# Decode attention on one core: pairwise additions on VectorE in place of half the score reductions on TensorE, with the statistics of an item moved behind the next item's first multiply

## The chip, the cores and the metric

One core of a Trainium2 chip. The metric is device time in microseconds (us) of one execution. The kernel before took 1992.97 us (median of 3 runs, 1991.46 to 1994.55).

## The reference

Two attention blocks, A and B, of the same shapes, one query token each; the results are put side by side.

```python
B, Sq, D = 2, 1, 640
H, Sk, Dh = 32, 8192, 192
q = (x @ wq)                       # per block; reshaped to (B, H, 1, Dh)
scores = einsum("bhqd,bhkd->bhqk", q, k_cache) * Dh ** -0.5
p = softmax(scores, axis=-1)
o = einsum("bhqk,bhkd->bhqd", p, v_cache)
out = o.reshape(B, Sq, H * Dh) @ wo          # concatenated over the two blocks
```

Everything is bf16. There are 2 x 2 x 32 = 128 pairs of a batch entry and a head. The kernel calls each pair an *item*. An item reads 8192 x 192 keys and as many values, 3 MB each, and uses every number once. 837 MB are loaded in all.

## The kernel before

Items are numbered 0 to 127 and fall into 8 groups of 16. Each K and V tile is 128 partitions x (64 x 192). K has 2 slots, V has 3. One queue (SyncE) issues all loads in order; a slot is loaded again when its former item has been used:

```python
for i in range(NH):                                   # SyncE
    # ... loads of wq and wo for a coming group at fixed items
    if i >= NK: sp.wait_ge(s_mul, NCH * (i - NK + 1)) # all 4 multiplies of item i-2
    sp.dma_start(kslot(i % NK), ...)
    if i >= NV: sp.wait_ge(s_pv, i - NV + 1)          # all value matmuls of item i-3
    sp.dma_start(vslot(i % NV), ...)
```

The scores of an item are formed by VectorE and TensorE together. VectorE multiplies K by the query, in four chunks of 48 of the 192 dimensions. TensorE sums the products by matmuls with an identity matrix that accumulate in PSUM, six per chunk, 24 per item, each folding the sum into 8 partial sums per key. VectorE adds the 8 (`sred_nrs`), takes the minimum of the negated scores per partition, TensorE transposes it (`maxt`), VectorE reduces it to the bias (`bias_op`), ScalarE takes the exponential, and TensorE multiplies by V in 32 matmuls (`pv_range`).

```python
def mul_chunk(i, c):                                  # VectorE, K x q for 48 dimensions
    # ... c == 0: wait for the K load
    if ci >= NP: dve.wait_ge(s_red, ci - NP + 1)
    dve.tensor_tensor(out=pslot(ci % NP)..., in0=kv[:, :, c*DCH:(c+1)*DCH],
                      in1=qv[...].broadcast_to([P, T, DCH]), op=ALU.mult).then_inc(s_mul, 1)

def red_chunk(p, c):                                  # TensorE: 6 matmuls of 128x512
    pe.wait_ge(s_mul, ci + 1)
    for j in range(MPC):
        mm = pe.matmul(S_ps[p % 2][:, 0:SN], lhsT=ident_b, rhs=pv_[:, :, j*D2:(j+1)*D2], ...)
    mm.then_inc(s_red, 1)

for i in range(NH):                                   # VectorE
    mul_chunk(i, 0); mul_chunk(i, 1)
    if gd is not None: group_end(gd)                  # normalise a finished group
    mul_chunk(i, 2); mul_chunk(i, 3)
    sred_nrs(i)
    bias_op(i)
    if gd is not None: mask_copy(gd)

for p in range(NH + 1):                               # TensorE, cut
    pv_range(p - 1, 0, 16)                            # value matmuls of the item before
    for c in range(NCH):
        red_chunk(p, c); pv_range(p - 1, u, u + 2); u += 2
    pv_range(p - 1, u, u + 4); u += 4
    maxt(p)
    pv_range(p - 1, u, TU)                            # the last 4
    # ... group-end transposes, query matmuls, projection
    # after the last item: pv_range(127, 0, 32), 14 matmuls to keep the clock up, transposes, projection
```

At the end of a group VectorE normalises the outputs, replicates them eight times under a mask (`o_rep`, 32 x 1536 fp32), and TensorE brings them into the layout of the projection by 12 fp32 matmuls against a 0/1 matrix. The profile counts 24 instructions for these.

## Time and profile before

| | before |
|---|---|
| time | 1992.97 us |
| DMA, share of its 16 engines' time | 98% |
| TensorE (PE) busy | 85% |
| VectorE (DVE) busy | 53% |
| loads, steady rate | about 429 GB/s |

Lines of the page of the kernel before: busy time and its share of the span by engine, three strips of 40 equal slices (granted TensorE clock in tenths, DMA share in tenths, GB/s), and the bytes read.

```profile
PE 1701.0 (85%) x8536; PEld 722.9 (36%) x8536; DVE 1058.0 (53%) x1084; ACT 91.0 (5%) x326; POOL 5.4 (0%) x17
...
PEclk9989999999899998999999999899999989999998
DMA  9999999999999999999999999999999999999993
GB/s 402 424 433 427 433 425 431 428 432 429 427 428 431 429 429 428 429 429 430 429 427 429 431 428 431 427 430 429 430 429 428 430 430 430 427 409 429 431 429 139
...
HBM read 836.77 MB, written 0.01 MB: 420 GB/s over the span
```

The DMA strip is at 9 (90% or more) in 39 of 40 slices. GB/s is flat near 430 apart from the first and the last slice and one at 409, which holds the end of the last group but one; we come back to it. These are groups of instructions of the same kernel: line, engine, operation, output and inputs with shapes, count, then busy us and mean ns of one, then the idle time of that engine just before them and what ended it.

```profile
L339 DVE TENSOR_TENSOR pbuf<-kbuf,qbc 128x3072 bf16<-128x3072 bf16 x512 | 866.2, 1753 | 488.1 <-DMA kbuf<-in_A_k_cache_dram 256.7
L514 PE MATMUL bank<-pbuf,ident_b 128*128 128x512 bf16 x3072 | 796.6, 398 | 272.0 <-DVE pbuf L339 272.0
...
L348 DVE TENSOR_REDUCE sc_sb<-bank 128x64 f32<-128x512 f32 x128 | 88.6, 692 | 338.0 <-PE bank L514 338.0
```

VectorE stood idle 488 us until a K tile landed, and 338 us until TensorE had finished a reduction. The loads do not wait for long. The list of load issues (count, size, median us from issue to landing) shows them queued well ahead:

```profile
kbuf<-in_A_k_cache_dram SPq DMA_DIRECT2D x64, 3072.0 KB, 22.5
vbuf<-in_A_v_cache_dram SPq DMA_DIRECT2D x64, 3072.0 KB, 25.4
```

A tile of 3 MB takes 7.3 us by itself at 429 GB/s. It lands 22.5 or 25.4 us after its issue, so 15 to 18 us of other loads stand ahead of it. Now the ending, from the timeline (start us, duration us, engine, line, operation, count, and in brackets the idle time before it and what ended it):

```profile
1941.46 6.76 DVE L339 TENSOR_TENSOR pbuf<-kbuf,qbc 128x3072 bf16<-128x3072 bf16 x4 [4.06 <-DMA kbuf<-in_B_k_cache_dram]
...
1956.07 6.76 DVE L339 TENSOR_TENSOR pbuf<-kbuf,qbc 128x3072 bf16<-128x3072 bf16 x4 [4.06 <-DMA kbuf<-in_B_k_cache_dram]
...
1968.79 5.37 PE L532 MATMUL bank<-vbuf,zwin 128*32 128x384 bf16 x32
...
1975.56 2.83 DVE L392 TENSOR_TENSOR o_rep<-tmpB,mask 32x1536 f32<-32x1536 f32 x1
...
1978.43 4.94 PE L578 MATMUL bank<-Sm_f,o_rep 32*128 32x16 f32 x24 [1.79 <-DVE o_rep L392]
...
1990.67 0.27 SPq L309 DMA_DIRECT2D out_dram<-out_sb  x1
```

K tiles are taken up 14.61 us apart (1941.46, 1956.07), each after a wait for DMA. That is 6.29 MB at 431 GB/s, the *beat* of the loads. After the last K come 36.1 us of tail to the end of the span: the last scores until 1968.79, the value matmuls, normalisation, the replicate (2.83 us), the transposes (4.94 us), the projection.

### The profile page before, as it was taken

What the parts mean: (1) busy time and instruction counts of PE and PEld (TensorE: products, weight loads), DVE (VectorE), ACT (ScalarE), POOL (GpSimd) and SP (SyncE); (2) the same over time, 40 slices, a digit from 0 to 9 for tenths busy, and PEclk for the clock granted to TensorE, in tenths of its full rate; (3) what the DMA queues carried; (4) which work ended last, traced back from release to release, by engine and by line L of the source; (5) the groups of instructions that cost most, each with busy time, mean ns of one, the idle gap of its engine ahead of it and who ended that gap; (6) DMA issues with size and microseconds to landing.
All of it is one profiled execution on the core that took longest, in us unless ns stands there. A gap on an engine that the chain in (4) does not pass through costs nothing.

```text
span 1992.2 us, 19490 instructions
## 1 busy us (share of the span) xinstructions
PE 1701.0 (85%) x8536; PEld 722.9 (36%) x8536; DVE 1058.0 (53%) x1084; ACT 91.0 (5%) x326; POOL 5.4 (0%) x17
## 2 busy tenths in 40 slices
PE   6869888888898888979888798887888889889888
PEld 2323333333333333333333333333333333343334
DVE  4545555545554555555455455554555555565553
ACT  1000000000000000000000000000000000000000
POOL 1000000000000000000000000000000000000000
PEclk9989999999899998999999999899999989999998
DMA  9999999999999999999999999999999999999993
GB/s 402 424 433 427 433 425 431 428 432 429 427 428 431 429 429 428 429 429 430 429 427 429 431 428 431 427 430 429 430 429 428 430 430 430 427 409 429 431 429 139
DMA packets 43366, 838.04 MB, mean 421 GB/s; under 512 B 4361, under 2 KB 4369, under 8 KB 9489
## 3 DMA queue, kind: packets, MB, share of 16 engines
q1 hardware_dynamic: 43280, 836.79, 98.3%
q8 instruction: 68, 1.11, 0.2%
q14 instruction: 18, 0.14, 0.0%
HBM read 836.77 MB, written 0.01 MB: 420 GB/s over the span
## 4 chain that ended last, share of the span: by engine, by line
DMA 74%; DVE 23%; PE 2%; issue 0%; SPq 0%; ACT 0%; ACTq 0%
DMA kbuf<-in_A_k_cache_dram 38%; DMA kbuf<-in_B_k_cache_dram 36%; DVE pbuf L339 21%; DVE o_rep L392 1%; PE bank L514 1%; PE bank L532 1%; PE bank L578 0%; PE bank L598 0%; DVE tmpB L383 0%; DVE tmpB L388 0%; DVE bank L399 0%; DVE rcpab L382 0%; PE bank L599 0%; PE bank L562 0%; DVE rcp L381 0%
## 5 line engine op out<-in xcount | busy, mean ns | idle before, releaser
L339 DVE TENSOR_TENSOR pbuf<-kbuf,qbc 128x3072 bf16<-128x3072 bf16 x512 | 866.2, 1753 | 488.1 <-DMA kbuf<-in_A_k_cache_dram 256.7
L514 PE MATMUL bank<-pbuf,ident_b 128*128 128x512 bf16 x3072 | 796.6, 398 | 272.0 <-DVE pbuf L339 272.0
L532 PE MATMUL bank<-vbuf,zwin 128*32 128x384 bf16 x4096 | 817.7, 334 | 2.5 <-ACT zwin L462 0.3
L514 PEld LDWEIGHTS bank<-pbuf,ident_b 128*128 128x128 bf16 x3072 | 268.0, 100 | 717.7 <-issue 419.9
L532 PEld LDWEIGHTS bank<-vbuf,zwin 128*32 128x32 bf16 x4096 | 338.4, 97 | 446.3 <-issue 256.0
L348 DVE TENSOR_REDUCE sc_sb<-bank 128x64 f32<-128x512 f32 x128 | 88.6, 692 | 338.0 <-PE bank L514 338.0
L462 ACT ACTIVATE zwin<-ns_sb,bias 128x64 bf16<-128x64 f32 x128 | 45.0, 352 | 1808.9 <-DVE bias L365 1808.9
L499 PE MATMUL bank<-wq_sb,xT 128*128 128x384 bf16 x320 | 64.5, 333 | 4.3 <-DMA wq_sb<-in_A_wq_dram 2.5
L365 DVE TENSOR_REDUCE bias<-bank 128x1 f32<-128x128 f32 x128 | 37.4, 292 | 53.7 <-PE bank L562 53.7
L562 PE MATMUL bank<-ident_f,nrs 128*128 128x128 f32 x128 | 41.1, 321 | 1.5 <-DVE ns_sb L356 1.0
L440 ACT ACTIVATE qbc<-bank 128x384 bf16<-128x384 f32 x64 | 31.4, 491 | 63.4 <-PE bank L499 63.4
L562 PEld LDWEIGHTS bank<-ident_f,nrs 128*128 128x128 f32 x128 | 17.0, 133 | 47.1 <-DVE ns_sb L356 44.1
L499 PEld LDWEIGHTS bank<-wq_sb,xT 128*128 128x128 bf16 x320 | 26.6, 99 | 19.9 <-issue 3.6
L540 PEld LDWEIGHTS bank<-ones_f,rz 128*32 128x32 f32 x256 | 28.2, 110 | 15.1
L598 PE MATMUL bank<-wo_sb,oM 128*2 128x512 bf16 x96 | 31.6, 403 | 0.5 <-DVE oM L406 0.5
L356 DVE TENSOR_SCALAR_CACHE_REDUCE ns_sb<-sc_sb 128x64 f32<-128x64 f32 x128 | 28.2, 220 | 4.4
L578 PE MATMUL bank<-Sm_f,o_rep 32*128 32x16 f32 x192 | 24.9, 270 | 1.8 <-DVE o_rep L392 1.8
L546 PE MATMUL bank<-ones_f,rz 128*32 128x1 f32 x256 | 25.8, 170 | 0.0
L540 PE MATMUL bank<-ones_f,rz 128*32 128x1 f32 x256 | 25.4, 168 | 0.0
L578 PEld LDWEIGHTS bank<-Sm_f,o_rep 32*128 32x128 f32 x192 | 24.1, 202 | 2.3 <-DVE o_rep L392 2.2
L462 ACT ACTIVATION_READ_ACCUMULATOR zwin<-ns_sb,bias 128x1 f32 x128 | 23.9, 187 | 0.0
L392 DVE TENSOR_TENSOR o_rep<-tmpB,mask 32x1536 f32<-32x1536 f32 x8 | 22.5, 2819 | 0.3
(40 smaller groups left out, 97.2 us busy)
## 6 DMA issues: line engine op xcount, KB each, us to landing
kbuf<-in_A_k_cache_dram SPq DMA_DIRECT2D x64, 3072.0 KB, 22.5
vbuf<-in_A_v_cache_dram SPq DMA_DIRECT2D x64, 3072.0 KB, 25.4
kbuf<-in_B_k_cache_dram SPq DMA_DIRECT2D x64, 3072.0 KB, 22.5
vbuf<-in_B_v_cache_dram SPq DMA_DIRECT2D x64, 3072.0 KB, 25.4
wq_sb<-in_A_wq_dram SPq DMA_DIRECT2D x4, 1920.0 KB, 30.1
wo_sb<-in_A_wo_dram SPq DMA_DIRECT2D x4, 1920.0 KB, 29.8
wq_sb<-in_B_wq_dram SPq DMA_DIRECT2D x4, 1920.0 KB, 29.5
wo_sb<-in_B_wo_dram SPq DMA_DIRECT2D x4, 1920.0 KB, 29.6
```

Source lines behind the costliest of these rows:

```text
L339: dve.tensor_tensor(out=pslot(ci % NP).rearrange("p (t d) -> p t d", d=DCH), in0=kv[:, :, c * DCH:(c + 1) * DCH], in1=qv[:, g % 2, hh, b, ...
L348: dve.tensor_reduce(out=sc_sb[:, (i % 2) * T:(i % 2 + 1) * T], in_=S_ps[i % 2][:, 0:SN].rearrange("p (t e) -> p t e", e=D2), axis=AX.X, op ...
L365: dve.tensor_reduce(out=bias[:, (i % 2):(i % 2) + 1], in_=MT_ps[:, 0:P], axis=AX.X, op=ALU.min,).then_inc(s_bias, 1)
L392: dve.tensor_tensor(out=o_rep[:, :].rearrange("m (j h q) -> m j h q", j=NJ, h=HG), in0=tmpB[:, :].rearrange("m (q j) -> m j q", j=NJ)[:, : ...
L462: act.activation(out=zs[:, :, C0:C0 + 2], in_=ns_sb[:, (p % 2) * T:(p % 2 + 1) * T].rearrange("p (u j) -> p u j", j=2), func=AF.Exp, bias= ...
L499: mm = pe.matmul(Q_ps[:, 0:QN], lhsT=xT[:, xo:xo + 1].broadcast_to([P, P]), rhs=wqv[:, dc, 2 * hp * Dh:2 * hp * Dh + QN], start=(dc == 0), ...
L514: mm = pe.matmul(S_ps[p % 2][:, 0:SN], lhsT=ident_b[:, :], rhs=pv_[:, :, j * D2:(j + 1) * D2], start=(c == 0 and j == 0), stop=(c == NCH - ...
L532: pe.matmul(O_ps[g % 2][0:R, 0:2 * Dh], lhsT=zs[:, u, C0 - 2 * m:C0 - 2 * m + R], rhs=vv[:, 2 * u:2 * u + 2, :], start=False, stop=False, ...
L540: pe.matmul(O_ps[g % 2][0:R, 2 * Dh:2 * Dh + 1], lhsT=rzs[:, RZC - 2 * m:RZC - 2 * m + R], rhs=ones_f[:, 0:1], start=False, stop=False, sk ...
L562: pe.transpose(out=MT_ps[:, 0:P], in_=nrs[:, (p % 2):(p % 2) + 1].broadcast_to([P, P]), identity=ident_f[:, :],).then_inc(s_maxt, 1)
L578: tr = pe.matmul(oT32_ps[:, j * G:(j + 1) * G], lhsT=o_rep[:, j * P:(j + 1) * P], rhs=Sm_f[:, :], start=True, stop=True,)
L598: pe.matmul(acc_ps1[0:Bsz, 0:512], lhsT=oMv[:, j, :], rhs=wov[:, j, 0:512], start=st, stop=sp_)
```

## The change

The intent is to take work off TensorE, the busiest compute engine. VectorE adds the product chunks in pairs, so TensorE reduces two half-size sets with 12 matmuls instead of four with 24. The statistics of item i move behind the first multiply of item i+1, so that VectorE works while TensorE reduces. The last four items take an "eager" path (`EAG`) in which statistics come first, and the very last item keeps the old four chunks (`LAST_PLAIN`). At group ends, the replicate becomes eight plain copies on ScalarE (one on VectorE for the last group), with the mask applied after the transposes. The 14 matmuls meant to keep TensorE's clock up are removed. The core of the diff. Cut are the schedules of the projection, which moves by one item, and of the wo loads, which move by two, and the construction of the new mask:

```diff
+    LAST_PLAIN = NH - 1 if NH >= 2 else -1
+    EAG = 4
@@ VectorE
+            def add_half(i, a):
+                dve.wait_ge(s_mul, NCH * i + 3 + a)
+                dve.tensor_tensor(
+                    out=pslot(a), in0=pslot(a), in1=pslot(a + 2), op=ALU.add,
+                ).then_inc(s_add, 1)
+            # item_seq(i): mul 0, mul 1, mul 2, add 0, mul 3, add 1; LAST_PLAIN: four multiplies
             for i in range(NH):
-                mul_chunk(i, 0)
-                mul_chunk(i, 1)
-                if gd is not None:
-                    group_end(gd)
-                mul_chunk(i, 2)
-                mul_chunk(i, 3)
-                sred_nrs(i)
-                bias_op(i)
+                if i >= NH - EAG:
+                    sred_nrs(i)
+                    bias_op(i)
+                    item_seq(i + 1)
+                    continue
+                item_seq(i + 1, hooks={
+                    1: before_stats + [lambda: sred_nrs(i)],
+                    2: [lambda: bias_op(i)] + after_bias,
+                })
@@ TensorE
+            def red_half(p, a):            # 6 matmuls on the sum of two chunks
@@
-                    pv_range(p - 1, 0, UH)
-                    for c in range(NCH):
-                        red_chunk(p, c)
-                        pv_range(p - 1, u, u + g1)
-                    ...
-                    maxt(p)
-                    pv_range(p - 1, u, TU)
+                        red_half(p, 0)
+                        pv_range(p - 1, 0, 12)
+                        red_half(p, 1)
+                        if eager:          # 6 value matmuls, maxt(p), the other 14
+                            ...
+                        else:
+                            pv_range(p - 1, 12, TU)
+                            maxt(p)
@@ after the last item
-                    warm(14)
```

More of the change, by code (lines that the diff above doesn't have):

```diff
@@ L71, in bass_concat_heads__gqa_block_cached__mha_block_cached__decode_kernel @@
     NK, NV, NP = 2, 3, 4
+    LAST_PLAIN = NH - 1 if NH >= 2 else -1
+    EAG = 4
+    assert G >= EAG + 4
+    assert NP == NCH == 4
     NPP = 4
@@ L100, in trans_iter, with mask_slot @@
         return min((g + 1) * G + 1, NH)
+    def mask_slot(g):
+        return min((g + 1) * G + 2, NH)
     proj_sched = {}
@@ L104, in bass_concat_heads__gqa_block_cached__mha_block_cached__decode_kernel @@
         for q in range(NPP):
-            p = min(trans_iter(g) + 1 + q, NH)
+            p = min((g + 1) * G + 3 + q, NH)
             proj_sched.setdefault(p, []).append((g, q))
@@ L109, in bass_concat_heads__gqa_block_cached__mha_block_cached__decode_kernel @@
         gl = (blk + 1) * NGB - 1
-        acc_sched[trans_iter(gl) + NPP] = blk
+        acc_sched[(gl + 1) * G + 3 + NPP] = blk
     sp_extra = {}
@@ L117, in bass_concat_heads__gqa_block_cached__mha_block_cached__decode_kernel @@
     for g in range(1, NG):
-        sp_extra.setdefault(g * G + 9, []).append(("wo", g))
+        sp_extra.setdefault(g * G + 11, []).append(("wo", g))
     for blk in range(NBLK - 1):
-        sp_extra.setdefault((blk + 1) * NGB * G + 12, []).append(("out", blk))
+        sp_extra.setdefault((blk + 1) * NGB * G + 14, []).append(("out", blk))
     es = contextlib.ExitStack()
@@ L144, in bass_concat_heads__gqa_block_cached__mha_block_cached__decode_kernel @@
         ones_f = sb("ones_f", [P, 1], F32)
-        mask2 = sb("mask2", [R, HG], F32)
+        mask_f = sb("mask_f", [P, G], F32)
+        ones_p = sb("ones_p", [P, G], F32)
+        tmpM = sb("tmpM", [P, NJ * G], F32)
         ones_r = sb("ones_r", [R, G], F32)
@@ L180, in bass_concat_heads__gqa_block_cached__mha_block_cached__decode_kernel @@
         s_mul = sem("s_mul")
+        s_add = sem("s_add")
         s_red = sem("s_red")
@@ L189, in bass_concat_heads__gqa_block_cached__mha_block_cached__decode_kernel @@
         s_ge = sem("s_ge")
+        s_o32 = sem("s_o32")
         s_onorm = sem("s_onorm")
@@ L250, in _ @@
             ).then_inc(s_pl, 1)
+            pool.memset(ones_p[:, :], 1.0).then_inc(s_pl, 1)
+            pool.wait_ge(s_pl, 6)
             pool.affine_select(
-                out=mask2[:, :], in_=ones_r[:, 0:HG], pattern=[[-4, HG]],
+                out=mask_f[:, :].rearrange("p (h b) -> p h b", b=Bsz),
+                in_=ones_p[:, :].rearrange("p (h b) -> p h b", b=Bsz),
+                pattern=[[-DQ, HG], [0, Bsz]],
                 compare_op=ALU.is_ge, fill=0.0, base=0, channel_multiplier=1,
             ).then_inc(s_pl, 1)
-            pool.wait_ge(s_pl, 6)
+            pool.wait_ge(s_pl, 7)
             pool.tensor_copy(out=ident_b[:, :], in_=ident_f[:, :]).then_inc(s_pl, 1)
@@ L261, in _ @@
             pool.affine_select(
-                out=mask2[:, :], in_=mask2[:, :], pattern=[[4, HG]],
-                compare_op=ALU.is_ge, fill=0.0, base=3, channel_multiplier=-1,
+                out=mask_f[:, :].rearrange("p (h b) -> p h b", b=Bsz),
+                in_=mask_f[:, :].rearrange("p (h b) -> p h b", b=Bsz),
+                pattern=[[DQ, HG], [0, Bsz]],
+                compare_op=ALU.is_ge, fill=0.0, base=DQ - 1, channel_multiplier=-1,
             ).then_inc(s_pl, 1)
@@ L267, in _ @@
             pool.memset(rz[:, :], 0.0).then_inc(s_pl, 1)
-            pool.wait_ge(s_pl, 12)
+            pool.wait_ge(s_pl, 13)
             pool.memset(rcp[:, :], 1.0).then_inc(s_const, 1)
@@ L336, in mul_chunk @@
                         qc_waited[0] = need
-                if ci >= NP:
-                    dve.wait_ge(s_red, ci - NP + 1)
+                if c < 2 and i >= 1:
+                    dve.wait_ge(s_red, 2 * (i - 1) + c + 1)
                 dve.tensor_tensor(
-                    out=pslot(ci % NP).rearrange("p (t d) -> p t d", d=DCH),
+                    out=pslot(c).rearrange("p (t d) -> p t d", d=DCH),
                     in0=kv[:, :, c * DCH:(c + 1) * DCH],
@@ L344, in mul_chunk @@
                 ).then_inc(s_mul, 1)
+            def add_half(i, a):
[3 more added lines that the diff above has]
+                ).then_inc(s_add, 1)
             def sred_nrs(i):
-                dve.wait_ge(s_red, NCH * (i + 1))
+                dve.wait_ge(s_red, 2 * (i + 1))
                 dve.tensor_reduce(
@@ L382, in group_end @@
                 step(dve.tensor_tensor(out=rcpab[:, :], in0=par[:, :], in1=rcp[:, 0:1].broadcast_to([R, 2]), op=ALU.mult))
+                if g >= 1:
+                    dve.wait_ge(s_onorm, g)
                 step(dve.tensor_scalar(
@@ L385, in group_end @@
                 ))
-                if g >= 1:
-                    dve.wait_ge(s_ot, g)
-                step(dve.scalar_tensor_tensor(
+                dve.scalar_tensor_tensor(
                     out=tmpB[:, :], in0=ops[0:R, 0:Dh], scalar=rcpab[:, 0:1], in1=tmpB[:, :],
                     op0=ALU.mult, op1=ALU.add,
-                ))
-                dve.tensor_tensor(
-                    out=o_rep[:, :].rearrange("m (j h q) -> m j h q", j=NJ, h=HG),
-                    in0=tmpB[:, :].rearrange("m (q j) -> m j q", j=NJ)[:, :, None, :].broadcast_to([R, NJ, HG, DQ]),
-                    in1=mask2[:, None, :, None].broadcast_to([R, NJ, HG, DQ]),
-                    op=ALU.mult,
-                ).then_inc(s_onorm, 1)
-                dve.wait_ge(s_onorm, g + 1)
+                ).then_inc(s_o32, 1)
+                dve.wait_ge(s_o32, g + 1)
+                if g == NG - 1:
+                    if g >= 1:
+                        dve.wait_ge(s_ot, g)
+                    dve.tensor_copy(
+                        out=o_rep[:, :].rearrange("m (j h q) -> m j h q", j=NJ, h=HG),
+                        in_=tmpB[:, :].rearrange("m (q j) -> m j q", j=NJ)[:, :, None, :].broadcast_to([R, NJ, HG, DQ]),
+                    ).then_inc(s_onorm, 1)
                 dve.memset(ops[0:R, 0:2 * Dh + 1], 0.0).then_inc(s_zero, 1)
@@ L402, in mask_copy @@
                 dve.wait_ge(s_ot, g + 1)
+                dve.tensor_tensor(
+                    out=tmpM[:, :].rearrange("p (j m) -> p j m", m=G),
+                    in0=oT32_ps.rearrange("p (j m) -> p j m", m=G),
+                    in1=mask_f[:, None, :].broadcast_to([P, NJ, G]),
+                    op=ALU.mult,
+                ).then_inc(s_ge, 1)
+                ge_cnt[0] += 1
+                dve.wait_ge(s_ge, ge_cnt[0])
                 if g >= 1:
@@ L407, in mask_copy, with item_seq @@
                         out=oM2[:, :].rearrange("p (j b) -> p j b", b=Bsz),
-                        in_=oT32_ps.rearrange("p (j h b) -> p j b h", j=NJ, h=HG),
+                        in_=tmpM[:, :].rearrange("p (j h b) -> p j b h", j=NJ, h=HG),
                         axis=AX.X, op=ALU.add,
                     ).then_inc(s_mc, 1)
-            for i in range(NH):
-                gd = (i - 2) // G if (i >= 2 and (i - 2) % G == G - 1) else None
-                mul_chunk(i, 0)
-                mul_chunk(i, 1)
-                if gd is not None:
-                    group_end(gd)
-                mul_chunk(i, 2)
-                mul_chunk(i, 3)
-                sred_nrs(i)
-                bias_op(i)
-                if gd is not None:
-                    mask_copy(gd)
+            def item_seq(i, hooks=None):
+                hooks = hooks or {}
+                steps = [
+                    lambda: mul_chunk(i, 0), lambda: mul_chunk(i, 1), lambda: mul_chunk(i, 2),
+                    lambda: add_half(i, 0), lambda: mul_chunk(i, 3), lambda: add_half(i, 1),
+                ]
+                if i == LAST_PLAIN:
+                    steps = [lambda c=c: mul_chunk(i, c) for c in range(NCH)]
+                for k, st in enumerate(steps):
+                    for h in hooks.get(k, []):
+                        h()
+                    st()
@@ new lines, in _ @@
+            item_seq(0)
+            for i in range(NH):
+                if i + 1 == NH:
+                    sred_nrs(i)
+                    bias_op(i)
+                    break
+                if i >= NH - EAG:
+                    sred_nrs(i)
+                    bias_op(i)
+                    item_seq(i + 1)
+                    continue
+                after_bias, before_stats = [], []
+                for g in range(NG):
+                    if (g + 1) * G == i:
+                        after_bias.append(lambda g=g: group_end(g))
+                    if mask_slot(g) == i:
+                        before_stats.append(lambda g=g: mask_copy(g))
+                item_seq(i + 1, hooks={
+                    1: before_stats + [lambda: sred_nrs(i)],
+                    2: [lambda: bias_op(i)] + after_bias,
+                })
@@ L424, in _ @@
             for g in range(NG):
-                if trans_iter(g) >= NH:
+                if (g + 1) * G >= NH:
                     group_end(g)
+                if mask_slot(g) >= NH:
                     mask_copy(g)
@@ L444, in q_copy, with replicate @@
                 ).then_inc(s_qc, 1)
+            def replicate(g):
+                act.wait_ge(s_o32, g + 1)
+                if g >= 1:
+                    act.wait_ge(s_ot, g)
+                orv = o_rep[:, :].rearrange("m (j h q) -> m j h q", j=NJ, h=HG)
+                src = tmpB[:, :].rearrange("m (q j) -> m j q", j=NJ)
+                for hh in range(HG):
+                    cp = act.activation(out=orv[:, :, hh, :], in_=src, func=AF.Copy)
+                cp.then_inc(s_onorm, 1)
             def fin_copy(blk):
@@ L469, in _ @@
                     q_copy(g, r)
+                for g in range(NG):
+                    if (g + 1) * G == p and p < NH:
+                        replicate(g)
                 if p in acc_sched:
@@ L505, in q_round, with red_quarter @@
                 mm.then_inc(s_qp, 1)
-            def red_chunk(p, c):
-                ci = NCH * p + c
+            def red_half(p, a):
+                if a == 0 and p >= 2:
+                    pe.wait_ge(s_sred, p - 1)
+                pe.wait_ge(s_add, 2 * p + a + 1)
+                pv_ = pslot(a).rearrange("p (t d) -> p t d", d=DCH)
+                for j in range(MPC):
+                    mm = pe.matmul(
+                        S_ps[p % 2][:, 0:SN],
+                        lhsT=ident_b[:, :],
+                        rhs=pv_[:, :, j * D2:(j + 1) * D2],
+                        start=(a == 0 and j == 0), stop=(a == 1 and j == MPC - 1),
+                    )
+                mm.then_inc(s_red, 1)
+            def red_quarter(p, c):
                 if c == 0 and p >= 2:
                     pe.wait_ge(s_sred, p - 1)
-                pe.wait_ge(s_mul, ci + 1)
-                pv_ = pslot(ci % NP).rearrange("p (t d) -> p t d", d=DCH)
+                pe.wait_ge(s_mul, NCH * p + c + 1)
+                pv_ = pslot(c).rearrange("p (t d) -> p t d", d=DCH)
                 for j in range(MPC):
@@ L519, in red_chunk @@
                     )
-                mm.then_inc(s_red, 1)
+                if c % 2 == 1:
+                    mm.then_inc(s_red, 1)
             def pv_range(i, u0, u1):
@@ L558, in maxt @@
                 for g in range(NG):
-                    if trans_iter(g) == p - 1:
+                    if trans_iter(g) < p <= mask_slot(g):
                         pe.wait_ge(s_mc, g + 1)
@@ L566, in maxt @@
                 ).then_inc(s_maxt, 1)
-            def warm(n):
-                for _ in range(n):
-                    pe.matmul(Q_ps[:, 0:QN], lhsT=ident_b[:, :], rhs=wqv[:, 0, 0:QN], start=True, stop=True)
             def out_transposes(g, p):
@@ L603, in _ @@
                 q_round(0, r)
+            n_a1 = max(1, (3 * TU) // 8)
+            n_a2 = (3 * TU) // 16
             g1 = max(1, TU // 16)
-            UH = TU // 2 if TU >= 16 else 0
-            assert UH + 6 * g1 <= TU
             for p in range(NH + 1):
@@ L609, in _ @@
                     u = 0
-                    if p >= 1 and UH:
-                        pv_range(p - 1, 0, UH)
-                        u = UH
-                    for c in range(NCH):
-                        red_chunk(p, c)
-                        if p >= 1:
-                            pv_range(p - 1, u, u + g1)
-                            u += g1
-                    if p >= 1:
-                        pv_range(p - 1, u, u + 2 * g1)
-                        u += 2 * g1
-                    maxt(p)
-                    if p >= 1:
-                        pv_range(p - 1, u, TU)
+                    eager = p >= NH - EAG and p >= 1
+                    if p == LAST_PLAIN and p >= 1:
+                        for c in range(NCH):
+                            red_quarter(p, c)
+                            hi = min(TU, u + (g1 if c < NCH - 1 else n_a2))
+                            if hi > u:
+                                pv_range(p - 1, u, hi)
+                                u = hi
+                        maxt(p)
+                        if u < TU:
+                            pv_range(p - 1, u, TU)
+                    else:
+                        red_half(p, 0)
+                        if p >= 1:
+                            hi = min(TU, u + n_a1)
+                            pv_range(p - 1, u, hi)
+                            u = hi
+                        red_half(p, 1)
+                        if eager and u < TU:
+                            hi = min(TU, u + n_a2)
+                            if hi > u:
+                                pv_range(p - 1, u, hi)
+                                u = hi
+                            maxt(p)
+                            if u < TU:
+                                pv_range(p - 1, u, TU)
+                        else:
+                            if p >= 1 and u < TU:
+                                pv_range(p - 1, u, TU)
+                            maxt(p)
                     for g in range(NG):
@@ L632, in _ @@
                     pv_range(p - 1, 0, TU)
-                    pe.wait_ge(s_qc, NQR * NG)
-                    warm(14)
                     for g in range(NG):
```

## The prediction

> **What bounds the kernel now.** The loads. The windows view shows the 16 DMA engines 0.99 to 1.01 busy at about 429 GB/s between the ends; 837 MB (queue table) at 429 GB/s is 1951 us of a 1992 us span. The chain of waits is 74% DMA. One item (3 MB of K, 3 MB of V) takes 14.6 us: in the timeline the K tiles of undisturbed items become usable that far apart (1941.46, 1956.07). In that time VectorE works about 8 us and waits some 4 us for K; TensorE's 85% is off the path. The Trainium skill, "DMA: Bandwidth & Descriptors", Specifications, puts the fabric ceiling at 435 GB/s; the trace agrees with 429 to 433.
>
> After the last K (1956.05) comes a tail of 36.1 us.
>
> **What the change does.**
> - It halves the score reduction on TensorE: 12 matmuls of 128x512 per item, not 24; about 2.8 us per item, 360 us in all.
> - It adds two 128x3072 bf16 additions per item on VectorE. Costed like the multiply (same shape and type, 1.75 us): about +445 us, so VectorE goes from 1058 to about 1490 us (75%). "VectorE: DVE Perf Modes", Mode 2x_1P, says a two-tensor 16-bit op with unit step can deliver two results a cycle; the multiply's 1.75 us agrees. About 11.7 us per item still fits in 14.6.
> - It moves the statistics of item i behind the first multiply of item i+1. Relative to a K landing, the K slot frees about 3 us later and the V slot about 6 us later. Issue to landing is now 22.5 us (K) and 25.4 us (V), 7.3 us of it the transfer itself. I expect about 19 us for both, leaving 12 us of backlog. At the last group boundary the old kernel already issued both 5 us late, yet later K landings kept the beat. So this should cost nothing.
> - At group ends the 2.8 us masked replicate moves to ScalarE (95% idle), and a mask multiply (about 0.3 us) is added: off the path, except at the end.
>
> **On the critical path.** Only the tail. The last item keeps four multiplies and four reductions. Previously 16 of item 126's value matmuls ran while waiting for the last K; now 20 of them, not 4, follow the last max transpose, at 0.167 us each: about +2.3 us, partly repaid (about 1 us) because TensorE should be warmer when the last reductions start. The last replicate becomes a plain copy, 1.2 to 1.6 us shorter; the mask multiply costs 0.35 us. Removing the 14 warm matmuls changes nothing: the transposes after them already ran at clock 0.55. Net about 0, within 2 us.
>
> **Predicted: 1993 us**, range 1986 to 2001. Faster by over 2%: 0.01; within 2%: 0.96; slower by over 2%: 0.03.
>
> **What the profile should show.** DMA still 0.99 busy at 429 GB/s; additions near 1.7 us; TensorE busy down by about 350 us, less if its clock falls; K and V issue to landing near 19 us; VectorE's waits for K well below 488 us; tail 34 to 39 us.
>
> **What would make it wrong.** Additions at half speed (3.3 us) would put VectorE at about 15 us per item, above the beat: slower by several per cent. Idle stretches could leave TensorE at half clock, near 14.6 us per item, delaying V until the queue runs dry. Over 2% faster would need more than 429 GB/s; I see no source for it.

## The result, and the profile after

The changed kernel took 1995.13 us (median of 10 runs, 1994.48 to 1996.08); the kernel before, beside it, 1993.0 us (12 runs, 1990.41 to 1994.57). The ratio is 1.0013, with a 95% interval of 1.0003 to 1.0022. Ratios here are the mean time of one kernel's runs over that of the other's of the same rounds, so not quite the ratio of the medians quoted. The verdict is "same": a difference of about 2 us, far inside 2%. The prediction had 1993 us, 1986 to 2001.

| | before | after |
|---|---|---|
| time, median | 1993.0 us | 1995.13 us |
| TensorE busy | 1701.0 us | 1474.7 us |
| VectorE busy | 1058.0 us | 1469.0 us |
| granted TensorE clock, mean | 0.955 | 0.836 |
| loads, mean over the span | 420 GB/s | 420 GB/s |

The same lines of the page, of the changed kernel:

```profile
PE 1474.7 (74%) x6998; PEld 689.0 (35%) x6998; DVE 1469.0 (74%) x1339; ACT 111.4 (6%) x382; POOL 5.6 (0%) x18
...
PEclk8888888888888888888878888788788888888888
DMA  9999999999999999999999999999999999999992
GB/s 402 425 433 429 429 426 432 430 428 430 426 430 430 430 429 428 430 430 429 431 426 430 430 430 430 424 427 431 428 430 426 427 430 429 430 419 431 429 431 120
```

The DMA strip and the GB/s are what they were, but for 419 in place of 409 in one slice. 411 us more of VectorE and 226 us less of TensorE changed neither. The groups of the changed kernel that answer to those above (L356 multiplies, L581 reduces on TensorE, L365 adds, L371 is the first statistics reduction):

```profile
L356 DVE TENSOR_TENSOR pbuf<-kbuf,qbc 128x3072 bf16<-128x3072 bf16 x512 | 896.7, 1753 | 436.2 <-DMA kbuf<-in_A_k_cache_dram 233.5
L581 PE MATMUL bank<-pbuf,ident_b 128*128 128x512 bf16 x1524 | 516.8, 491 | 448.7 <-DVE pbuf L365 448.7
...
L365 DVE TENSOR_TENSOR pbuf<-pbuf 128x3072 bf16<-128x3072 bf16 x254 | 446.5, 1758 | 8.7
...
L371 DVE TENSOR_REDUCE sc_sb<-bank 128x64 f32<-128x512 f32 x128 | 87.6, 685 | 19.0 <-PE bank L581 16.6
```

An addition takes 1.758 us, the multiply 1.753 us. VectorE's wait for TensorE before its first statistics reduction went from 338 to 19 us: the additions, and the next item's first multiply that now stands ahead of the statistics, fill that wait. Its wait for K fell only from 488 to 436 us. The reductions are half as many but cost 0.491 us each in the profile, not 0.398. TensorE now idles 449 us before them, and its clock has dropped when they start: near the end, for one, a set of six takes 2.72 us at 1949.47, and the granted clock from 1950 to 1954 us is 0.50.

The load issues of the changed kernel land sooner after their issue, because slots come free later and the queue ahead is shorter:

```profile
kbuf<-in_A_k_cache_dram SPq DMA_DIRECT2D x64, 3072.0 KB, 19.7
vbuf<-in_A_v_cache_dram SPq DMA_DIRECT2D x64, 3072.0 KB, 18.5
```

The ending, in the timeline of the changed kernel:

```profile
1942.45 5.08 DVE L356 TENSOR_TENSOR pbuf<-kbuf,qbc 128x3072 bf16<-128x3072 bf16 x3
...
1956.92 0.69 DVE L371 TENSOR_REDUCE sc_sb<-bank 128x64 f32<-128x512 f32 x1 [4.13 <-PE bank L581]
...
1958.50 6.76 DVE L356 TENSOR_TENSOR pbuf<-kbuf,qbc 128x3072 bf16<-128x3072 bf16 x4
...
1972.30 5.36 PE L614 MATMUL bank<-vbuf,zwin 128*32 128x384 bf16 x32
...
1979.05 1.49 DVE L419 COPY o_rep<-tmpB 32x1536 f32<-32x1536 f32 x1
...
1980.60 4.08 PE L656 MATMUL bank<-Sm_f,o_rep 32*128 32x16 f32 x24 [2.84 <-DVE o_rep L419]
...
1991.38 0.27 SPq L326 DMA_DIRECT2D out_dram<-out_sb  x1
```

The multiplies of item 127 (1958.50) no longer show a wait for DMA. Before them VectorE stood 4.13 us at L371, waiting for TensorE's reduction of item 126. In this eager ending the statistics of an item are waited for before the next multiply, and from 1942.45 to 1958.50 an item takes 16.05 us, more than the beat. When the last K landed doesn't show in these lines, since nobody was waiting for it. The view of its load issue has it: issued at 1936.0,

```profile
DMA to landing us min/median/max: 17.8/17.8/17.8
```

so it had landed by 1953.8, 2.3 us sooner than in the kernel before, and was taken up 4.7 us late. The replicate shrank to 1.49 us.

### The profile page after: what moved, and what is told of

Read it like the earlier page. It is cut to its first block, busy times and chain, and to the rows that moved or that the text cites. A ratio compares the mean times of both kernels' runs of the same rounds, so it can differ in the third digit from the quotient of the medians. Undisturbed runs are those within 1.5% of the kernel's fastest.

```text
span 1992.9 us, 16733 instructions
## 1 busy us (share of the span) xinstructions
PE 1474.7 (74%) x6998; PEld 689.0 (35%) x6998; DVE 1469.0 (74%) x1339; ACT 111.4 (6%) x382; POOL 5.6 (0%) x18
## 4 chain that ended last, share of the span: by engine, by line
DMA 46%; DVE 26%; PE 24%; issue 4%; SPq 0%; ACT 0%; ACTq 0%
DMA kbuf<-in_A_k_cache_dram 25%; DMA kbuf<-in_B_k_cache_dram 21%; DVE pbuf L356 15%; PE bank L614 14%; PE bank L581 8%; DVE pbuf L365 7%; DVE sc_sb L371 2%; DVE bias L388 1%; PE bank L656 1%; PE bank L644 1%; DVE ns_sb L379 1%; PE bank L595 0%; PE bank L676 0%; PE bank L628 0%; DVE tmpB L411 0%
## 5 line engine op out<-in xcount | busy, mean ns | idle before, releaser
L356 DVE TENSOR_TENSOR pbuf<-kbuf,qbc 128x3072 bf16<-128x3072 bf16 x512 | 896.7, 1753 | 436.2 <-DMA kbuf<-in_A_k_cache_dram 233.5
L581 PE MATMUL bank<-pbuf,ident_b 128*128 128x512 bf16 x1524 | 516.8, 491 | 448.7 <-DVE pbuf L365 448.7
L614 PEld LDWEIGHTS bank<-vbuf,zwin 128*32 128x32 bf16 x4096 | 409.8, 105 | 463.5 <-issue 268.0
L365 DVE TENSOR_TENSOR pbuf<-pbuf 128x3072 bf16<-128x3072 bf16 x254 | 446.5, 1758 | 8.7
L581 PEld LDWEIGHTS bank<-pbuf,ident_b 128*128 128x128 bf16 x1524 | 153.4, 113 | 716.6 <-issue 635.7
L371 DVE TENSOR_REDUCE sc_sb<-bank 128x64 f32<-128x512 f32 x128 | 87.6, 685 | 19.0 <-PE bank L581 16.6
L567 PEld LDWEIGHTS bank<-wq_sb,xT 128*128 128x128 bf16 x320 | 35.2, 111 | 20.4 <-issue 5.0
L656 PE MATMUL bank<-Sm_f,o_rep 32*128 32x16 f32 x192 | 31.0, 306 | 13.1 <-DVE bias L388 10.3
L656 PEld LDWEIGHTS bank<-Sm_f,o_rep 32*128 32x128 f32 x192 | 30.4, 246 | 14.4 <-issue 11.4
L508 ACT ACTIVATE o_rep<-tmpB 32x192 f32<-32x192 f32 x56 | 24.8, 524 | 4.4 <-DVE tmpB L411 4.4
```

The costliest lines, as they stand in the source:

```text
L356: dve.tensor_tensor(out=pslot(c).rearrange("p (t d) -> p t d", d=DCH), in0=kv[:, :, c * DCH:(c + 1) * DCH], in1=qv[:, g % 2, hh, b, :][:, ...
L365: dve.tensor_tensor(out=pslot(a), in0=pslot(a), in1=pslot(a + 2), op=ALU.add,).then_inc(s_add, 1)
L371: dve.tensor_reduce(out=sc_sb[:, (i % 2) * T:(i % 2 + 1) * T], in_=S_ps[i % 2][:, 0:SN].rearrange("p (t e) -> p t e", e=D2), axis=AX.X, op ...
L567: mm = pe.matmul(Q_ps[:, 0:QN], lhsT=xT[:, xo:xo + 1].broadcast_to([P, P]), rhs=wqv[:, dc, 2 * hp * Dh:2 * hp * Dh + QN], start=(dc == 0), ...
L581: mm = pe.matmul(S_ps[p % 2][:, 0:SN], lhsT=ident_b[:, :], rhs=pv_[:, :, j * D2:(j + 1) * D2], start=(a == 0 and j == 0), stop=(a == 1 and ...
L614: pe.matmul(O_ps[g % 2][0:R, 0:2 * Dh], lhsT=zs[:, u, C0 - 2 * m:C0 - 2 * m + R], rhs=vv[:, 2 * u:2 * u + 2, :], start=False, stop=False, ...
```

## The experiments

Two theories of why nothing moved:

- **T: the loads are the floor.** Both kernels hide their compute behind 429 GB/s, and only the tail after the last K differs.
- **R: two effects cancel.** The relief of TensorE helps and something in the steady part (a shorter load queue, a lower clock, VectorE's added work) takes it back.

Each experiment was timed beside the kernel before on the same chip.

### Only the loads

All compute is removed; each load is issued again when the former one in its slot has landed. The result is wrong.

```diff
-                if i >= NK:
-                    sp.wait_ge(s_mul, NCH * (i - NK + 1))
+                if i >= NK:
+                    sp.wait_ge(s_k[i % NK], 16 * (i // NK))
     # the same for V, wq, wo; TensorE, ScalarE, GpSimd and VectorE (but for one memset) removed
```

> Only the loads, in the same order into the same slots, each reissued as soon as the slot's former load has landed; no compute (wrong result on purpose). Theory T (the loads are the floor): 1950 to 1965 us, about 429 GB/s, so 30 to 40 us below both kernels, which is the tail after the last loads. Rival (the kernels hold the loads back): below 1930 us.

Measured: 1954.7 us (one look). The page of this kernel:

```profile
GB/s 406 426 432 431 430 427 431 428 433 431 427 431 429 432 432 427 431 430 429 433 427 429 432 429 433 427 429 432 428 433 427 430 432 429 433 428 433 428 432 389
...
HBM read 836.76 MB, written 0.01 MB: 428 GB/s over the span
```

The loads alone need 1954.7 us, 98% of both kernels' times, at 428 GB/s. What either kernel can still win is at most the 38 to 40 us above that. Most of it is the tail: in the kernel before, the last V lands at 1963.65 and 28.5 us follow. A part is lost in the loads themselves: by 1940 us this run had moved about 3.1 MB more than the kernel before (sums of the traces' packets), which is 7 us at 430 GB/s.

### The compute of both kernels without later loads

K and V are loaded once per slot and then used again and again (wrong result); all else stays.

```diff
-                if i >= NK:
-                    sp.wait_ge(s_mul, NCH * (i - NK + 1))
-                sp.dma_start(kslot(i % NK), ...).then_inc(s_k[i % NK], 16)
+                if i < NK:
+                    sp.dma_start(kslot(i % NK), ...).then_inc(s_k[i % NK], 16)
+                else:
+                    sp.wait_ge(s_mul, NCH * (i - NK + 1))
     # the same for V; VectorE and TensorE wait for 16 on s_k and s_v
```

The kernel before:

> The kernel before without the loads of K and V after the first in each slot (wrong result on purpose): what its compute costs alone. Theory T: in the one stretch of the trace where it did not wait for loads an item took 12.55 us, so about 128 x 12.5 plus group ends and tail: 1650 to 1720 us, some 280 us below the time with loads. Rival (TensorE at 85% busy was itself nearly the limit): above 1900 us.

The changed kernel:

> The changed kernel without the loads of K and V after the first in each slot (wrong result on purpose). Theory T (from the one stretch without load waits, bias to bias 14.19 us): 1800 to 1880 us, so slower than the kernel before when compute alone counts, and only about 0.4 us per item below the beat of the loads. Rival (as the prediction summed VectorE, 11.7 us per item): about 1550 to 1600 us, and faster than the kernel before without loads.

Measured (one look each): 1693.93 us for the kernel before, as expected; 1895.54 us for the changed kernel, 15 us above the expected range. Alone, the changed kernel's compute is 202 us *slower*, though it does half the reductions. The page of the kernel before without later loads shows why its compute is where it is: TensorE is full.

```profile
PE 1650.1 (98%) x8536; PEld 713.6 (42%) x8536; DVE 1046.7 (62%) x1084; ACT 91.0 (5%) x326; POOL 5.3 (0%) x17
```

For the changed kernel, the timeline without later loads, one item from bias to bias (L390):

```profile
1005.22 0.29 DVE L390 TENSOR_REDUCE bias<-bank 128x1 f32<-128x128 f32 x1 [1.08 <-PE bank L646]
...
1009.12 2.72 PE L583 MATMUL bank<-pbuf,ident_b 128*128 128x512 bf16 x6 [3.03 <-DVE pbuf L367]
...
1014.04 1.47 PE L583 MATMUL bank<-pbuf,ident_b 128*128 128x512 bf16 x6
...
1015.44 3.42 PE L616 MATMUL bank<-vbuf,zwin 128*32 128x384 bf16 x20
...
1018.89 0.32 PE L646 MATMUL bank<-ident_f,nrs 128*128 128x128 f32 x1
...
1019.25 0.29 DVE L390 TENSOR_REDUCE bias<-bank 128x1 f32<-128x128 f32 x1 [1.08 <-PE bank L646]
```

An item takes 14.03 us, though neither engine is full. The six reductions at 1009.12 start after an idle gap of 3.03 us and take 2.72 us where the next six (1014.04) take 1.47. Twelve value matmuls lie between the two halves and twenty between the second half and the transpose (1018.89), on which the bias waits. The bias in turn holds up the next multiply and addition. It is a ring of waits through both engines, and it is only 0.6 us shorter than the beat of 14.61 us.

### Is it that ring?

On top of the changed kernel without later loads, TensorE puts the max transpose of every item ahead of the last 14 value matmuls. The eager ending does this already.

```diff
-                    eager = p >= NH - EAG and p >= 1
+                    eager = p >= 1
```

> The changed kernel without the later loads of K and V (wrong result on purpose), and on TensorE the max transpose of each item put 14 value matmuls earlier (as the eager ending has it). Theory T (without loads its loop is a chain: additions, first half reduction at half clock, 12 value matmuls, second half, 20 value matmuls, transpose, bias, next multiply): the chain loses about 2.3 us and VectorE's sum of about 12.2 us becomes the limit: an item 12.2 to 12.7 us, 1650 to 1720 us in all, against 1895.5. Rival (VectorE's sum plus fixed waits is the limit already): above 1850 us.

Measured: 1588.14 us (one look), 307 us less than 1895.54 and below the expected range. One moved instruction per item is worth more without loads than the whole change cost. VectorE is now 92% busy, so its sum is close to the limit. The ring accounts for the 202 us and more.

Then the same edit on the changed kernel with all its loads:

> The changed kernel with all its loads, and the max transpose of every item put 14 value matmuls earlier on TensorE: the edit that took 307 us off its compute when the later loads were left out (1895.5 to 1588.1). Theory T (the loads are the floor, compute alone is hidden behind them): the time stays where it is, 1991 to 1997 us. Rival (the compute loop of 14.03 us matters somewhere in the steady part): 1985 us or less.

Measured: 1993.42 us (4 runs, 1992.87 to 1994.8) against 1991.43 for the kernel before, ratio 1.0009 [0.9993, 1.0024]. 307 us less compute left the time where it was. With the loads running, compute of either length is hidden. This is what separates T from R most clearly: under R a gain of this size in the steady part should have shown.

### How much more VectorE work is free

One, two and three dead additions per item are put after the second addition of the changed kernel; results stay right. With n the number (a wait of the third multiply for the dead additions is cut):

```diff
                     out=pslot(a), in0=pslot(a), in1=pslot(a + 2), op=ALU.add,
                 ).then_inc(s_add, 1)
+                if a == 1:
+                    for _ in range(n):
+                        if dead[0]: dve.wait_ge(s_dead, dead[0])
+                        dve.tensor_tensor(out=pslot(2), in0=pslot(2), in1=pslot(3), op=ALU.add).then_inc(s_dead, 1)
+                        dead[0] += 1
```

One:

> The changed kernel with one more (dead) 128x3072 bf16 addition per item on VectorE, after the second addition; results unchanged. VectorE's own work per item goes from about 12.2 to 13.9 us. Theory T (the loads set the beat at 14.61 us, and the 14.03 us loop that the changed kernel shows without loads runs through TensorE and the statistics, not through VectorE's sum): no change, 1993 to 1998 us. Rival (an addition lengthens the 14.03 us loop itself, to about 15.7 us): 2070 us or more.

Two:

> The changed kernel with two more dead additions per item. VectorE's sum per item becomes about 15.7 us, over the 15.2 us that the loads need on average (837 MB over 128 items at 429 GB/s). Theory T: now VectorE is the limit, 16 us start + 127 x 15.7 + 20 us of group ends + 36 us tail: 2060 to 2120 us, DMA share down to about 0.93, VectorE's waits for K near zero. Rival (VectorE has more room than that): below 2010 us.

Three:

> The changed kernel with three more dead additions per item. With two, the trace shows VectorE setting the pace at 14.80 us per item (bias to bias, no wait), so the changed kernel itself needs 14.80 - 2 x 1.72 = about 11.4 us of VectorE per item, not the 12.2 us assumed for the last two runs; the weights' loads (73 us in all) hid the 0.2 us per item. Theory T: with three the pace is 16.5 us: 16 us start + 127 x 16.5 + 16 us of group ends + 36 us tail, 2130 to 2180 us, clearly slower. Rival (additions hide behind something else still): below 2030 us.

Measured: 1996.16 us with one (4 runs, ratio 1.0019 [1.0004, 1.0034] to the kernel before), 1998.45 us with two (one look), 2177.85 us with three (one look). The expectation for two was a miss, by 60 us and more. The text behind it took VectorE's sum as 12.2 us per item. The traces give the right one: with two additions the bias instructions follow each other without a wait at

```profile
1842.49 0.28 DVE L400 TENSOR_REDUCE bias<-bank 128x1 f32<-128x128 f32 x1
...
1857.28 0.28 DVE L400 TENSOR_REDUCE bias<-bank 128x1 f32<-128x128 f32 x1
```

14.79 us, and with three at

```profile
1004.31 0.28 DVE L400 TENSOR_REDUCE bias<-bank 128x1 f32<-128x128 f32 x1
...
1020.89 0.28 DVE L400 TENSOR_REDUCE bias<-bank 128x1 f32<-128x128 f32 x1
```

16.58 us. The step is 1.79 us per addition, so the changed kernel needs 14.79 - 2 x 1.79 = 11.2 us of VectorE per item. The prediction had said 11.7. With two additions VectorE is 95% busy and its pace is 0.18 us slower per item than the beat; the loads of the weights, which ask nothing per item of VectorE, hide that. With three it is over, and the time follows. So additions on VectorE cost little here until its own sum passes the loads' time.

### The ending: where the 2 us are

In the changed kernel, `EAG = 4` becomes 0: items 124 to 126 keep the normal order.

```diff
-    EAG = 4
+    EAG = 0
```

> The changed kernel with its eager ending switched off (EAG = 0 instead of 4: items 124 to 126 keep the normal order, statistics after the first multiply of the next item). Theory T (only the tail differs; the eager ending makes VectorE serial at about 16 us per item and starts the last item's multiplies about 4.5 us after its K landed): the first multiply of item 127 then waits for the DMA and starts near 1954; the time falls by 2 to 4 us against the changed kernel, to about 1991 to 1993, level with or just below the kernel before. Rival R (the 2 us came from the steady part: shallower load queue or lower TensorE clock): no change, about 1995.

Measured: 1992.38 us (5 runs, 1992.25 to 1993.33) against 1992.93 for the kernel before, ratio 1.0 [0.9986, 1.0014]. Now the last item's first multiply waits for its K again. The timeline of this run:

```profile
1954.01 1.76 DVE L356 TENSOR_TENSOR pbuf<-kbuf,qbc 128x3072 bf16<-128x3072 bf16 x1 [3.20 <-DMA kbuf<-in_B_k_cache_dram]
...
1969.33 5.36 PE L614 MATMUL bank<-vbuf,zwin 128*32 128x384 bf16 x32
```

The last K was there by 1954.01; the changed kernel had multiplied it at 1958.50. The last value matmuls start at 1969.33, not at 1972.30. The expected 2 to 4 us are there by the medians (1995.13 to 1992.38). These two kernels were timed in different sessions, and their intervals against the kernel before overlap, so the times alone don't prove it; the 4.5 us in the trace, from 1958.50 to 1954.01, are plain. The span fell by only 1.3 us (1992.9 to 1991.6). TensorE's half-speed stretch in the tail fell otherwise in this run: the transposes took 5.15 us at a granted clock of 0.52, against 4.08 us at 0.67.

### Towards a faster version: only the ending of the kernel before

If the loads are the floor, the kernel to start from is the one with the shorter tail and the larger reserve. In the kernel before, the last K is issued ahead of item 126's V; item 127's first multiplies come before item 126's statistics; and on TensorE item 127's reductions come before item 126's value matmuls.

```diff
@@ SyncE
+                if i == NH - 2: continue            # V of item 126 later
+                if i == NH - 1: ...                 # after the last K: V of item 126, then V of item 127
@@ VectorE
+                # item 126: its four multiplies, mul_chunk(127, 0), sred_nrs(126), mul_chunk(127, 1),
+                # bias_op(126), mul_chunk(127, 2), mul_chunk(127, 3)
@@ TensorE
+                    if p == NH - 1:
+                        for c in range(NCH): red_chunk(p, c)
+                        pv_range(p - 1, 0, 6)
+                        maxt(p)
+                        pv_range(p - 1, 6, TU)
```

> The kernel before with another ending only: the last K is issued ahead of V of item 126, item 127's first multiplies come before the statistics of item 126, and on TensorE the four reductions of item 127 come before item 126's value matmuls. Theory T (only the tail is left to win; the loads stay): last value matmuls start near 1964.5 instead of 1968.8, total about 4 us less, 1988 to 1990 us. Rival (the last V or V of item 126 then lands too late and TensorE waits for it): 1992 us or more.

Measured: 1988.17 us (5 runs, 1987.11 to 1990.81) against 1991.61, ratio 0.9982 [0.997, 0.9995]. The last value matmuls start at 1964.35 in the trace, as expected.

Next, `o_rep` and the 0/1 matrix are held in bf16, on top of that:

```diff
-        o_rep = sb("o_rep", [R, NJ * P], F32)
+        o_rep = sb("o_rep", [R, NJ * P], BF16)
-                        rhs=Sm_f[:, :],
+                        rhs=Sm_b[:, :],             # bf16 copy of Sm_f
```

> The ending of the previous run (last K first, reductions first) plus replicated outputs and the summing matrix held in bf16 instead of fp32, so that 12 matmuls take the place of the 24 in the transposes of each group end. Theory T: the 4.99 us of transposes at half clock in the tail become 1.5 to 2.5 us, total 1985 to 1987 us. Rival (the tail's length is set elsewhere): same as the previous run, 1988 us.

And the changed kernel's plain replicate for the last group, with the mask after the transposes:

> The same, plus the changed kernel's plain copy for the last group's replicate with the mask applied after the transposes (2.83 us become 1.49 us, and 0.38 us are added). Theory T: about 1 us less again, 1984 to 1986 us. Rival: no further gain.

Measured: 1983.28 us (5 runs, 1982.45 to 1983.53), ratio 0.9954 [0.9941, 0.9966]; and 1981.79 us (5 runs, 1980.91 to 1983.22), ratio 0.995 [0.9936, 0.9963]; the kernel before took 1991.56 in both. Both are correct. The first gained more than expected. From the timeline of the last version:

```profile
1963.89 5.36 PE L590 MATMUL bank<-vbuf,zwin 128*32 128x384 bf16 x32
...
1970.64 1.52 DVE L421 CAST o_rep<-tmpB 32x1536 bf16<-32x1536 f32 x1
...
1972.22 0.45 PE L636 MATMUL bank<-Sm_b,o_rep 32*128 32x16 bf16 x12 [0.48 <-DVE o_rep L421]
...
1973.10 0.35 DVE L450 TENSOR_REDUCE oM<-tmpM 128x24 bf16<-128x192 f32 x1
...
1977.83 0.27 SPq L337 DMA_DIRECT2D out_dram<-out_sb  x1
```

The transposes take 0.45 us, not 4.94. The projection starts half a microsecond after 1973.10 and is over by 1977.0, in 3.4 us instead of 6.0, because the clock no longer falls. Windows of the granted clock (the number before the last two of each line), the kernel before first, then the last version:

```profile
1976.65:1978.40 1.75, 0.00 (x0) 0.00 (x0) 1.73 (x1) 0.00 (x0) 0.00 (x0) 1.00 0.00 0
1978.40:1983.40 5.00, 4.94 (x24) 4.83 (x24) 0.38 (x1) 0.00 (x0) 0.00 (x0) 0.55 0.00 0
```

```profile
1972.20:1972.70 0.50, 0.45 (x12) 0.36 (x12) 0.38 (x1) 0.00 (x0) 0.00 (x0) 1.00 0.00 0
1973.60:1977.00 3.40, 3.40 (x24) 1.62 (x24) 0.00 (x0) 0.00 (x0) 0.00 (x0) 1.00 0.00 0
```

This version keeps the old steady loop, which leaves 98% of the time untouched, and is 9.8 us faster than the kernel before beside it; the changed kernel's median of another session is 13 us higher. By the profiled runs it comes from the tail: the last value matmuls start 4.9 us sooner (1963.89, not 1968.79) and from there to the end it takes 15.5 us, not 23.4. The bf16 transposes serve the other seven group ends too; what they bring there was not separated.

## Why the prediction was right

- **The loads bound the kernel.** Shown: loads alone take 1954.7 us; 307 us of compute taken away changed nothing; one extra addition per item left the ratio to the kernel before at 1.0019, within the noise of the 1.0013 without it.
- **Costs.** Additions were put at 1.75 us and took 1.758. VectorE was to reach 1490 us and reached 1469. K and V were to land about 19 us after issue and took 19.6 and 18.3 (means of the medians for A and B). TensorE was to lose 350 us, "less if its clock falls": it lost 226, and the mean clock fell from 0.955 to 0.836.
- **"About 11.7 us per item still fits in 14.6."** The sum was right (11.2 by the runs with additions), but the reading was not: the compute loop is a ring of 14.03 us, not the sum of one engine. The reserve was 0.6 us, not 2.9. The prediction held because the ring still fitted, which was luck: it had not looked at the ring, and with a beat under 14.03 us the ring would have set the pace. Its claim that VectorE's waits for K would fall "well below 488 us" also failed: they fell to 436, since the additions went mostly into the 338 us in which VectorE had waited for TensorE.
- **The tail, "net about 0, within 2 us".** By the two profiled runs it was +0.7 us (1992.2 to 1992.9), by the medians +2.1, just outside. From the traces, the terms that the prediction had came close: from the last K's first multiply to the last value matmuls 13.8 us instead of 12.7, +1.1 (predicted +1.3, that is 2.3 less 1); the replicate -1.34; the mask multiply, with its gap, +0.4. Together +0.2. It lacked three others: the last K lands 2.3 us sooner (1953.8, not 1956.05); VectorE takes it up 4.7 us late, because of the eager ending; and the transposes (4.08 us, not 4.94) and the projection (4.97, not 5.96) are 1.9 us shorter, since the half-clock stretch falls otherwise. Together +0.5. That these nearly cancel is luck.
- **The last group boundary.** The prediction read the late issues there in the old kernel as costing nothing. They did cost loads. Windows of 40 us at that boundary, the kernel before and then the changed kernel (the last numbers are the granted clock, the DMA share and GB/s):

```profile
1740.00:1780.00 40.00, 34.84 (x183) 16.21 (x182) 24.33 (x29) 1.32 (x6) 0.00 (x0) 0.91 0.95 401
```

```profile
1740.00:1780.00 40.00, 33.16 (x165) 16.90 (x163) 29.87 (x34) 4.43 (x12) 0.00 (x0) 0.83 0.99 417
```

  Against 430 GB/s that is a loss of about 2.7 us and 1.2 us (estimates from these figures). So by this estimate about 1.5 of the 2.3 us by which the last K lands sooner were won there.
- **Open.** Which part of the change helps at the group boundary, and where the rest of the 2.3 us comes from, was not tested. The 14 removed matmuls were not tested alone. That the clock holds with bf16 transposes was seen in two versions, and not separated into fewer matmuls, shorter time and type.

## What to carry to other kernels

When the DMA strip is full from end to end, work moved between compute engines hardly shows, however busy the relieved engine looked, as long as each item's compute stays within the time of its loads (three extra additions, at 16.58 us per item, no longer did). Measure the loads alone first: what remains above them is the most that can be won. A loop's compute time is the longest ring of waits through all engines, not always the sum of its busiest one, and it shows only when the loads are taken away: here a change that halved one engine's reductions, added additions on another and reordered the statistics made the hidden loop 202 us slower. In the tail, by contrast, a microsecond on the path to the end counts: order the last loads by what is needed first, and look there for the small operations that run at half clock.

## What the Trainium skill lacked or had wrong

- "DMA: Bandwidth & Descriptors", Where 436 GB/s comes from, says that for transfers between HBM and SBUF the HBM side, about 358 GB/s per core, binds. The sentence leaves out the condition that a note above it gives, that both cores of the pair stream; the sentence after it calls the page's own single-core 425 GB/s near the fabric rate. With one core running, the loads from HBM alone moved 428 GB/s over 1953 us; the page's fabric ceiling of 435 GB/s is the one that fits.
- "VectorE: DVE Perf Modes", The perf-mode tier table, lists fp32 `tensor_copy` in SBUF at 2x. The replicate (32 x 1536 fp32, source stepping by 12 elements and repeated eight times) took 1.49 us, which is 1.03 elements per ns, close to 1x at the page's 0.96 GHz; 2x would be about 0.8 us (an estimate, 1536 / 2 / 0.96). The table has no row for such strides and repeats.
- "TensorE: Matmul & The Clock Gate", What's actually happening, gives about 3.4 us of idleness as what halves the clock. In the tail of the kernel before, the clock was granted at 0.55 during 4.94 us of back-to-back fp32 matmuls (32 x 16 moving data) after a pause of only 1.79 us; in the second of the faster versions, with 12 bf16 matmuls after a pause of the same 1.79 us, it stayed at 1.00. The section does not say whether such small fp32 matmuls count as activity, and no run here settles it.
